# Fused channel attention and FFN on one core: the read-back of lines of maxima and the additions behind W_in loads are put a period later

## The chip, the cores and the metric

One core of a Trainium2 chip. The metric is device time in microseconds (us) of one execution; three runs of the kernel before have a median of 2120.12 us. Lower is better.

## What is computed

q, k and v have the shape (4, 6080, 256); W_in is 256 x 2048, W_out 2048 x 256, both stored as float64, and the outputs are compared in float32. The reference, cut:

```python
qn = q / (norm(q, axis=1) + 1e-6); kn = k / (norm(k, axis=1) + 1e-6)
s = kn.transpose(0, 2, 1) @ qn / tau          # (4, 256, 256)
a = softmax(s, axis=-1)
x = (v @ a).reshape(24320, 256)               # tokens
h = x @ w_in
return maximum(0.01 * h, h) @ w_out
```

The kernel doesn't form x: for each batch b it multiplies the small matrix a into W_in (`w_pair`), and then sends v through that product, the leaky step and W_out.

## The kernel before

**Tiles and periods.** The tokens of a batch are cut into six tiles (`NT`) of twice 512 or twice 496 tokens, 24 tiles in all. For each tile i, the main loop at the end of the kernel runs over eight pairs p of blocks of the 2048 hidden columns. One pass of its body is a period; the number of the period, i * 8 + p, stands in `now[0]`. In each period TensorE makes the products of one pair (`block_product` into the banks `ps_x`, `ps_y`, `ps_z`; a Strassen-Winograd scheme of seven block products, each split in three passes of high and low parts), and in between, in pieces by `out(5)`, `out(5)`, `out(8)` and the remaining six, the 24 products with W_out of the period before (`ffn_out`, bank `ps_o`). ScalarE copies sums out of the banks (`taken`, L827), makes the leaky step and the high halves (`leaky`, L809 and L812); VectorE adds into `h` (`add`, L821) and makes the low halves (L814). At the end of a tile four results `o_sb` are copied (L864) and stored to `out_dram` on SyncE (L874).

**The order of the work.** `in_order` pins the order of TensorE, ScalarE and VectorE to that in which the Python code calls the operations. Side work goes through queues: `at(w, fn)` has a function called at the start of period w; `put(queue, length, fn, then)` appends an operation to an engine's list `todo`; `slot(queue, room)` lets waiting operations into a gap of the period, first in first out, as far as their lengths fit the room. `put_steps` chains operations: each is put when the one before it has been issued; an entry "call" only calls a function. An entry for "act_next" reaches ScalarE's list at the start of the next period. DMAs on SyncE are not pinned: the framework's scheduler orders that queue when the program is compiled, and SyncE then works through it in this order, waiting in front of each DMA for what it needs.

**Lines of maxima (`Scale`).** From period 40 on, the operands are float16, scaled by a power of two. For this the greatest magnitude is needed: `see` gives it per partition (L141), and `gather` (L146 to L149) reduces it to a column of 128 values, writes the column to a line in DRAM and reads the line back, broadcast to all partitions, into a buffer `all`. `find` (L154 on) makes the scales of it. There are twenty such lines: one of `wo_scale` (found in period 24), one of `w_scale` (gathered at the end of the second `sums_work`, found in period 33) and eighteen of `v_scale` (`v_scale_work`: for tile i + 1 gathered in the second period of tile i and found at the start of its fourth).

**Sums of W_in blocks (`sums_work`).** In period 9 for q = 0 and in period 17 for q = 1, four blocks of W_in are loaded from DRAM (`win_in`, L962), added and subtracted on VectorE (`whole` L974, `minus` L981), their maxima taken (`seen`), split in high and low (`halves`: L986 on ScalarE, L990 on VectorE) and stored to `win_sums` (L991); later periods use them in `w_pair`. A first pair of blocks is loaded when `sums_work` is called, which puts the steps in the same breath; a second pair by `more`, behind the low half of block 0.

**Shared buffers.** `win` tiles, the chunks `qk_raw` of queries and keys, and the converted weights share a ring of four buffers with the tag "raw" (`RBUFS`). In periods 8 to 27 the chunks of batch 1 pass through it, to be squared on ScalarE (L217) and added up on VectorE (L220). `h`, `o_sb`, `all`, `sq` and others share twelve buffers with the tag "temp" (`TEMPS`); a buffer of `o_sb` comes free when its store has landed.

Of the kernel before, what the change touches and what calls it, by code (L numbers as in the profile page):

```python
# [36 lines left out]
def channel_attention_ffn(  # L37
# [29 lines left out]
    if N % TILE:  # L67
        rest = N % TILE // 2 + (widths.pop() if widths else 0)
# [18 lines left out]
    def temp(dtype=F32, name="temp"):  # L87
        return work.tile([P, TW], dtype, name=name, tag="temp", bufs=TEMPS)
# [32 lines left out]
    def f32(ap):  # L121
        return ap if ap.dtype == F16 else ap.bitcast(F32)
# [5 lines left out]
    class Scale:  # L128
# [16 lines left out]
        def gather(self):  # L145
            last = nc.vector.tensor_reduce(out=self.top, in_=self.most, axis=AX.X, op=ALU.max)  # L146
            nc.sync.dma_start(out=self.line, in_=self.top)
            self.all = temp(name="all")[:, 0:P]
            nc.sync.dma_start(out=self.all, in_=self.line.rearrange("p o -> (p o)").partition_broadcast(P))  # L149
            return last  # L150

        def find(self):
            e = self.e.bitcast(I32)
# [16 lines left out]
    class Scores:  # L170
# [10 lines left out]
        def begin(self, acc, *s):  # L181
            self.acc, self.s = acc, s
# [333 lines left out]
    def flat(w):  # L516
        return f32(w.rearrange("p x f -> p (x f)"))
# [40 lines left out]
    def w_tmp(name):  # L558
        return work.tile([P, TW], F32, name=name, tag="w_tmp", bufs=8)
# [7 lines left out]
    now, w_done, w_stores = [0], {}, []  # L567
# [315 lines left out]
    def at(w, fn, *args):  # L883
        steps.setdefault(w, []).append((fn, args))
# [10 lines left out]
    def put(queue, length, fn, then=(), first=False, ready=lambda: True):  # L895


        def run():
            ins = fn()
            for entry in then:  # L900
                if entry[0] == "call":
                    entry[1](*entry[2:])
                else:
                    put(*entry)
            return ins

        run.ready = ready
        (todo[queue].appendleft if first else todo[queue].append)((length, run))
# [51 lines left out]
    def win_in(src):  # L960
        r = win_tile(False)
        nc.sync.dma_start(out=flat(r), in_=src)  # L962
        return r

    def sums_work(q):

        blocks = {(h, x): win_in(win_dram[2 * q + x][h]) for h, x in ((0, 1), (0, 0))}
        t = {}

        def whole(name, h, x):  # L970
            def fn():
                r = blocks[h, x]
                t[name] = w_tmp("win_s")
                return nc.vector.tensor_tensor(out=t[name], in0=f32(r[:, 0, :]), in1=f32(r[:, 1, :]), op=ALU.add)  # L974
            return ("dve", 0.7, fn)

        def seen(h, x):
            return ("dve", 0.7, lambda: w_scale.see(f32(blocks[h, x][:, 0, :])))

        def minus(out, x, y):  # L980
            return ("dve", 0.7, lambda: nc.vector.tensor_tensor(out=t[out], in0=t[x], in1=t[y], op=ALU.subtract))  # L981

        def halves(name, x):
            def high():
                t[name, 0] = work.tile([P, 2, TW], F32R, name="win_t", tag="qk_split", bufs=3)
                return nc.scalar.copy(out=t[name, 0][:, 0, :], in_=t[name])  # L986

            def low():
                r = t[name, 0]
                ins = nc.vector.tensor_tensor(out=r[:, 1, :], in0=t[name], in1=f32(r[:, 0, :]), op=ALU.subtract)  # L990
                nc.sync.dma_start(out=win_sums[q][x], in_=flat(r))  # L991
                return ins
            return [("act_next", 0.65, high), ("dve", 0.7, low)]

        def more():
            for h, x in ((1, 1), (1, 0)):
                blocks[h, x] = win_in(win_dram[2 * q + x][h])

        put_steps([
            whole("a", 0, 1), seen(0, 1), whole("b", 0, 0), seen(0, 0), minus("b", "a", "b"), *halves("b", 0),  # L1000
            ("call", more),
            whole("c", 1, 1), seen(1, 1), minus("a", "c", "a"), *halves("a", 2), minus("c", "c", "b"),
            *halves("c", 1), whole("d", 1, 0), seen(1, 0), minus("d", "d", "c"), *halves("d", 3),
            *([("dve", 0.2, w_scale.gather)] if q else []),
        ], False, False)

    A_S1, A_S2, A_S3, A_S4, A_11, A_12, A_22 = range(7)

# [87 lines left out]
    def put_steps(steps, first, on=True):  # L1096

        def entry(n):
            then = [entry(n + 1)] if n + 1 < len(steps) else ()
            if steps[n][0] == "call":  # L1100
                return ("call", lambda: (steps[n][1](*steps[n][2:]), *(put(*x) for x in then)))
            return (*steps[n], then, first or n > 0 and on)

        put(*entry(0))
# [70 lines left out]
    for pair in range(NWC // 2):  # L1175
        at(9 + 8 * pair, sums_work, pair)
# [196 lines left out]
    last = None  # L1373
    for i in range(NTILES):
        for p in range(NPAIR):
# [14 lines left out]
            if last is not None:  # L1390
                leaky(i, p - 1, "C12", last, last)
                last = None
# [41 lines left out]
            else:  # L1434
                last = h12
# [33 lines left out]
```

## Time and profile before

| | us |
|---|---|
| median of 3 runs | 2120.12 |
| the runs, from to | 2119.97 to 2120.28 |
| the profiled execution, device time | 2117.38 |
| its span, first to last instruction | 2115.6 |
| TensorE busy | 2093.8 |
| VectorE busy | 1594.4 |
| ScalarE busy | 1473.1 |

The times of all rows below are from the one profiled execution and count from the start of its span. PE is TensorE, DVE VectorE, ACT ScalarE, SPq the DMA queue of SyncE. A line of the timeline gives the start, the duration, the engine, the line of the code, the operation and its tiles, and in brackets how long the engine was idle before it and for whom it waited. A wait is given to the releaser that came last.

### The profile page before, as it was taken

The numbers are of one execution on the slowest core, as the hardware profiler recorded it, in microseconds if no ns is written. First come the engines' busy times: TensorE is split into PE (matmuls) and PEld (weight loads), VectorE is DVE, ScalarE is ACT, GpSimd is POOL, SyncE is SP. The second block draws the span as 40 slices with busy tenths as digits, with TensorE's granted clock in tenths as the row PEclk, the third lists the DMA queues.
The fourth block names the chain that finished last, engine by engine and source line by source line (L and its number), as shares of the span: only waits on it lengthen the run. The fifth ranks groups of instructions, "written<-read, shape, count | busy, mean of one in ns | idle before, by whom it ended". The sixth has DMA issues, their size and how long they took to land.

```text
span 2115.6 us, 27081 instructions
## 1 busy us (share of the span) xinstructions
PE 2093.8 (99%) x9656; PEld 1214.5 (57%) x9656; DVE 1594.4 (75%) x2905; ACT 1473.1 (70%) x2571; POOL 3.3 (0%) x11
## 2 busy tenths in 40 slices
PE   9999999999999999999999999999999999999999
PEld 8887877788875555544444545554444444444444
DVE  7988887777788777877878877777788766666654
ACT  6576777666667777766667777776666666666666
POOL 0000000000000000000000000000000000000000
PEclk9999999999999999999999999999999999999999
DMA  9946665444643333322534333232343222222220
GB/s 363 395 169 204 205 232 191 165 149 160 219 143 104 116 114 105 102 102 86 174 112 135 114 105 115 95 111 73 125 150 99 82 77 80 65 84 72 65 72 29
DMA packets 120167, 283.46 MB, mean 134 GB/s; under 512 B 15072, under 2 KB 40160, under 8 KB 120032
## 3 DMA queue, kind: packets, MB, share of 16 engines
q1 hardware_dynamic: 119664, 281.41, 39.2%
q8 instruction: 76, 1.25, 0.3%
q14 instruction: 59, 0.48, 0.1%
q10 hardware_dynamic: 368, 0.32, 0.1%
HBM read 227.93 MB, written 53.75 MB: 133 GB/s over the span
## 4 chain that ended last, share of the span: by engine, by line
PE 86%; DVE 7%; ACT 5%; DMA 1%; issue 1%; ACTq 0%
PE ps_o L847 40%; PE ps_x L798 21%; PE ps_z L798 15%; PE ps_s L250 4%; DVE h L821 2%; PE ps_o L250 2%; ACT h L809 2%; ACT g_split L812 2%; DVE g_split L814 2%; PE ps_y L250 2%; PE ps_s L1030 1%; ACT h L827 1%; DVE v_split L754 1%; DMA win<-win_dram 0%; DMA out_dram<-o_sb 0%
## 5 line engine op out<-in xcount | busy, mean ns | idle before, releaser
L847 PE MATMUL ps_o<-g_split,w_out_split 128*128 128x512 f16 (+3 forms) x4608 | 1124.7, 380 | 0.0
L814 DVE TENSOR_TENSOR g_split<-h,g_split 128x512 f16<-128x512 f32 (+3 forms) x768 | 524.9, 684 | 285.4 <-ACT g_split L812 270.6
L798 PE MATMUL ps_x<-v_split,w_split 128*128 128x512 f16 (+3 forms) x2304 | 628.0, 381 | 7.2 <-ACT h L827 6.8
L809 ACT ACTIVATE h<-h 128x512 f32<-128x512 f32 (+1 forms) x576 | 360.9, 627 | 326.6 <-DVE h L821 326.4
L847 PEld LDWEIGHTS <-w_out_split 128*128 128x128 f16 x3456 | 337.9, 98 | 400.2
L821 DVE TENSOR_TENSOR h<-ps_z,h 128x512 f32<-128x512 f32 (+1 forms) x568 | 386.6, 681 | 191.4 <-ACT h L827 185.7
L827 ACT COPY h<-ps_x 128x512 f32<-128x512 f32 (+1 forms) x576 | 333.2, 579 | 230.7 <-PE ps_x L798 221.9
L798 PEld LDWEIGHTS <-w_split 128*128 128x128 f16 x3024 | 288.4, 98 | 356.5 <-issue 37.1
L812 ACT CAST g_split<-h 128x512 f16<-128x512 f32 (+3 forms) x768 | 471.9, 615 | 23.6
L798 PE MATMUL ps_z<-v_split,w_split 128*128 128x512 f16 (+3 forms) x1680 | 456.3, 380 | 8.2 <-DVE h L821 6.6
L847 PEld LDWEIGHTS ps_o<-g_split,w_out_split 128*128 128x128 f32 x1152 | 217.2, 189 | 44.2
L798 PEld LDWEIGHTS ps_x<-v_split,w_split 128*128 128x128 f32 x576 | 107.9, 189 | 29.7 <-ACT h L827 7.4
L809 ACT ACTIVATE h<-ps_x 128x512 f32<-128x512 f32 (+1 forms) x192 | 112.8, 587 | 7.0 <-PE ps_x L798 6.6
L220 DVE TENSOR_TENSOR sq_acc<-sq_acc,sq 128x512 f32<-128x512 f32 x141 | 96.5, 684 | 0.4
L798 PEld LDWEIGHTS ps_z<-v_split,w_split 128*128 128x128 f32 x408 | 76.1, 189 | 24.2 <-DVE h L821 9.5
L217 ACT ACTIVATE sq<-qk_raw 128x512 f32<-128x512 f32 x141 | 87.2, 630 | 0.0
L754 DVE SCALAR_TENSOR_TENSOR v_split<-v_raw,v_scale,v_split 128x512 f16<-128x512 f32 (+1 forms) x107 | 79.8, 746 | 3.8
L250 PE MATMUL ps_s<-qk_split 128*128 128x512 f32 x192 | 73.2, 391 | 0.0
L229 DVE TENSOR_TENSOR qk_split<-qk_raw,qk_split 128x512 fp32r<-128x512 f32 x96 | 65.6, 684 | 0.0
L250 PE MATMUL ps_y<-qk_split 128*128 128x512 f32 x192 | 60.4, 337 | 0.0
L225 ACT CAST qk_split<-qk_raw 128x512 fp32r<-128x512 f32 x96 | 59.0, 615 | 0.0
L752 DVE TENSOR_SCALAR v_split<-v_raw,v_scale 128x512 f16<-128x512 f32 (+1 forms) x107 | 51.0, 477 | 0.0
(165 smaller groups left out, 1024.7 us busy)
## 6 DMA issues: line engine op xcount, KB each, us to landing
w_split<-w_dram SPq DMA_DIRECT2D x144, 448.0 KB, 3.9
w_split<-w_dram SPq DMA_DIRECT2D x40, 896.0 KB, 4.7
qk_raw<-in_q_dram SPq DMA_DIRECT2D x115, 256.0 KB, 4.8
qk_raw<-in_k_dram SPq DMA_DIRECT2D x115, 256.0 KB, 5.4
v_raw<-in_vT_dram SPq DMA_DIRECT2D x32, 512.0 KB, 4.8
out_dram<-o_sb SPq DMA_DIRECT2D x64, 256.0 KB, 4.4
win<-win_dram SPq DMA_DIRECT2D x26, 512.0 KB, 3.6
win<-win_sums SPq DMA_DIRECT2D x24, 512.0 KB, 3.3
```

What stands on the lines that cost most here:

```text
L217: return nc.scalar.activation(out=out, in_=self.chunk(j), func=AF.Square)
L220: return nc.vector.tensor_tensor(out=self.acc[0], in0=self.acc[0], in1=sq, op=ALU.add)
L229: return nc.vector.tensor_tensor(out=sp[:, :, 1, :], in0=self.chunk(j), in1=f32(sp[:, :, 0, :]), op=ALU.subtract)
L250: mm = nc.tensor.matmul(out=out, lhsT=lhsT, rhs=rhs, start=start, stop=stop, skip_group_check=True)
L754: return nc.vector.scalar_tensor_tensor(out=sp[:, 1, 0:w], in0=src, scalar=up, in1=sp[:, 0, 0:w], op0=ALU.mult, op1=ALU.subtract)
L798: mm = nc.tensor.matmul(out=ps[:, 0:n], lhsT=w[:, x, a, :], rhs=sp[:, y, 0:n], start=first and k == 0, stop=k == 2, skip_group_check=True,)
L809: nc.scalar.activation(out=out[:, 0:n], in_=h[:, 0:n], func=AF.Prelu, alpha=0.01, scale=G_SCALE if i >= T16 else 1.0)
L812: issued["act"] = nc.scalar.copy(out=sp[:, 0, 0:n], in_=out[:, 0:n])
L814: issued["dve"] = nc.vector.tensor_tensor(out=sp[:, 1, 0:n], in0=out[:, 0:n], in1=f32(sp[:, 0, 0:n]), op=ALU.subtract)
L821: issued["dve"] = nc.vector.tensor_tensor(out=h[:, 0:n], in0=ps[:, 0:n], in1=h[:, 0:n], op=ALU.add)
L827: issued["act"] = nc.scalar.copy(out=h[:, 0:n], in_=ps[:, 0:n])
L847: issued["pe"] = nc.tensor.matmul(out=o_ps[i][j][h][:, 0:n], lhsT=wo_lhsT(i, x, f, h), rhs=sp[:, y, 0:n], start=p == 0 and early and k == ...
```

## The change

Two edits. In `Scale`, the read-back of a line leaves `gather` and becomes a function `read` of its own, which is called at the start of the period after the one in which `gather` was issued. In `sums_work`, the loads of the first pair stay where they are, but the steps on it are put at the start of the next period (`begin`); the loads of the second pair (`more`) are called right behind the second `seen`, and the steps on that pair (`rest`) are put at the start of the period after the one in which the low half of block 0 was issued. The steps themselves and their order are the same.

```diff
@@ -145,9 +145,12 @@
         def gather(self):
             last = nc.vector.tensor_reduce(out=self.top, in_=self.most, axis=AX.X, op=ALU.max)
             nc.sync.dma_start(out=self.line, in_=self.top)
+            at(now[0] + 1, self.read)
+            return last
+
+        def read(self):
             self.all = temp(name="all")[:, 0:P]
             nc.sync.dma_start(out=self.all, in_=self.line.rearrange("p o -> (p o)").partition_broadcast(P))
-            return last
@@ -996,13 +999,18 @@
-        put_steps([
-            whole("a", 0, 1), seen(0, 1), whole("b", 0, 0), seen(0, 0), minus("b", "a", "b"), *halves("b", 0),
-            ("call", more),
+        def begin():
+            put_steps([
+                whole("a", 0, 1), seen(0, 1), whole("b", 0, 0), seen(0, 0), ("call", more),
+                minus("b", "a", "b"), *halves("b", 0), ("call", lambda: at(now[0] + 1, put_steps, rest, False, False)),
+            ], False, False)
+
+        rest = [
             whole("c", 1, 1), seen(1, 1), minus("a", "c", "a"), *halves("a", 2), minus("c", "c", "b"),
             *halves("c", 1), whole("d", 1, 0), seen(1, 0), minus("d", "d", "c"), *halves("d", 3),
             *([("dve", 0.2, w_scale.gather)] if q else []),
-        ], False, False)
+        ]
+        at(now[0] + 1, begin)
```

## Rows read from the trace of the kernel before

**Rows 1.** Page, part 1: TensorE's busy us (share of the span), instructions.

```profile
PE 2093.8 (99%) x9656; PEld 1214.5 (57%) x9656; DVE 1594.4 (75%) x2905; ACT 1473.1 (70%) x2571; POOL 3.3 (0%) x11
```

**Rows 2.** Waits of TensorE, whole span: us in total, times, longest us.

```profile
PE ps_x L798 <- ACT h L827: 6.8, 3, 6.0
PE ps_z L798 <- DVE h L821: 6.6, 7, 2.6
```

**Rows 3.** Timeline of TensorE: the eight `ps_o` products, once in each period.

```profile
194.56 1.98 PE L847 MATMUL ps_o<-g_split,w_out_split 128*128 128x512 f32 x8
207.72 2.00 PE L847 MATMUL ps_o<-g_split,w_out_split 128*128 128x512 f32 x8
217.94 1.98 PE L847 MATMUL ps_o<-g_split,w_out_split 128*128 128x512 f32 x8
...
279.29 1.98 PE L847 MATMUL ps_o<-g_split,w_out_split 128*128 128x512 f32 x8
292.23 2.00 PE L847 MATMUL ps_o<-g_split,w_out_split 128*128 128x512 f32 x8
...
365.19 1.98 PE L847 MATMUL ps_o<-g_split,w_out_split 128*128 128x512 f32 x8
384.31 1.98 PE L847 MATMUL ps_o<-g_split,w_out_split 128*128 128x512 f32 x8
```

**Rows 4.** Windows: stretch, us, each engine's busy us, granted clock, DMA share, GB/s.

```profile
372.50:379.00 6.50, 5.86 (x14) 4.59 (x15) 4.66 (x7) 4.20 (x7) 0.00 (x0) 0.51 0.72 262
```

**Rows 5.** Chain that ended last, in three stretches: start us, us, what.

```profile
191.39 6.41 DMA win<-win_dram
...
278.96 3.94 DMA win<-win_dram
...
362.97 9.46 DMA out_dram<-o_sb
```

**Rows 6.** Timeline of VectorE: steps of `sums_work`, and `gather` of `w_scale`.

```profile
191.59 0.68 DVE L974 TENSOR_TENSOR win_s<-win 128x512 f32<-128x512 f32 x1
197.82 0.69 DVE L974 TENSOR_TENSOR win_s<-win 128x512 f32<-128x512 f32 x1 [3.51 <-DMA win<-win_dram]
208.03 0.68 DVE L990 TENSOR_TENSOR win_t<-win_s,win_t 128x512 fp32r<-128x512 f32 x1
...
352.67 0.15 DVE L146 TENSOR_REDUCE w_scale<-w_scale 128x1 f32<-128x8 f32 x1
```

**Rows 7.** Timeline of ScalarE, 352 to 382 us: the first `o_sb`, the late `h`.

```profile
357.91 0.58 ACT L864 COPY o_sb<-ps_o 128x512 f32<-128x512 f32 x1
...
372.51 0.59 ACT L827 COPY h<-ps_x 128x512 f32<-128x512 f32 x1 [7.15 <-DMA out_dram<-o_sb]
```

**Rows 8.** Timeline of SyncE's DMA queue: a second-pair load; the line of `w_scale`.

```profile
199.14 0.33 SPq L962 DMA_DIRECT2D win<-win_dram  x1
...
352.85 0.33 SPq L147 DMA_DIRECT2D w_scale_line<-w_scale  x1
362.08 0.33 SPq L149 DMA_DIRECT2D all<-w_scale_line  x1
...
362.97 3.15 SPq L874 DMA_DIRECT2D out_dram<-o_sb  x3
```

**Rows 9.** Timeline of SyncE's DMA queue: a chunk's load, a `v_scale` read-back.

```profile
216.10 0.33 SPq L198 DMA_DIRECT2D qk_raw<-in_q_dram  x1
...
985.31 0.33 SPq L149 DMA_DIRECT2D all<-v_scale_line  x1
```

**Rows 10.** Timeline of ScalarE: squares of chunks of batch 1.

```profile
226.48 1.15 ACT L217 ACTIVATE sq<-qk_raw 128x512 f32<-128x512 f32 x2
```

**Rows 11.** Page, part 6: issues, KB each, median us from issue to landing.

```profile
all<-v_scale_line SPq DMA_DIRECT2D x18, 64.0 KB, 5.4
```

**Rows 12.** Tile `out_dram`, 185 to 195 us: the landing of four stores.

```profile
DMA to landing us min/median/max: 6.3/6.5/6.7
```

**Rows 13.** Timeline of VectorE: the `find` that reads the line of 985.31.

```profile
992.34 0.28 DVE L154 TENSOR_REDUCE v_scale<-all 128x1 f32<-128x128 f32 x1
```

## The prediction

> **What bounds the kernel now.** I read the page's busy times first. TensorE is busy for 2093.8 us, 99% of the span [rows 1]; no edit here takes an instruction from it, so only its idle time and its slow stretches can be won: some 22 us at most. Next, its waits [rows 2]: 6.8 us in 3 waits on ScalarE's copies of `ps_x`, 6.0 of it in one, and 6.6 us in 7 waits on VectorE's additions to `h`, 2.6 the longest. To see where these lie and what they cost in all, I took the TensorE timeline and one mark in each period: the start of the eight `ps_o` products, which every period has once. An ordinary period is 217.94 - 207.72 = 10.22 us. Three are longer [rows 3]: 13.16 (194.56 to 207.72), 12.94 (279.29 to 292.23) and 19.12 us (365.19 to 384.31). Over the ordinary period that is 2.94, 2.72 and 8.90, together 14.56 us. I price by marks and not by the waits, because the third wait of 6.0 us costs 2.9 more than itself: right behind it the granted clock is 0.51, the lower level, for 6.5 us [rows 4]; the first two waits have no such tail. The periods are numbered as in `now[0]`: tile 1 begins with period 8, and the three are 9, 17 and 25.
>
> Then each of the three followed back, with the chain of waits [rows 5] and the timelines of the engines.
>
> Periods 9 and 17: in both, the chain goes through the landing of the second `win` load of `sums_work`. It is issued at 191.39 and lands at 197.80; in period 17, at 278.96 and 282.90 [rows 5]. VectorE runs its queue in a fixed order. It has the first addition `win_s` done at 191.59, comes to the second and stands 3.51 us for the load [rows 6]; behind it stand the additions to `h`, for which `ps_z` and so TensorE wait. The pair of loads is called in the very period of the additions.
>
> Period 25: ScalarE stands 7.15 us before a copy to `h`, for a `temp` buffer whose store of `o_sb` hasn't landed [rows 7]. That store was issued at 362.97 [rows 8] and landed at 372.43 [rows 5], though its first `o_sb` was copied by 357.91 + 0.58 = 358.49 [rows 7]. Between, the DMA queue of SyncE was parked: the line of `w_scale` was written at 352.85, its read-back waited behind it until 362.08 for that write to land, and the stores stood behind the read-back [rows 8]. So one line in twenty costs time, because it falls on a tile's end.
>
> **The loads a period ahead.** The first pair keeps its place in the text, period 9 (17); the additions are put into VectorE's queue one period later. Nothing is computed more or less: 0 us of work. In the period after, the first addition comes at about 191.59 + 10.22 = 201.8, and the load is in at 197.80: 4 us to spare. In period 17, the mark of 18 without the stall is 279.29 + 10.22 = 289.5, the addition 3 us before it (as 191.59 is before 194.56), so 286.5 against 282.90: 3.6 us to spare. Both waits go: -2.94 and -2.72. The second pair is called after the second `seen`, and its users follow one period after `low` of block 0, so it's ahead too; it makes no wait now.
>
> What the move costs is in the ring of four `raw` buffers, which `win` shares with the query and key chunks of batch 1. Two `win` tiles now keep their buffers a period longer, and the second two between one and two. No row prices that. From below it is nothing: the loads go into buffers that squares free. From above: the load at 216.10 [rows 9] goes out as the second pair's first buffer comes free; it lands some 3.9 us later by the nearest row [rows 5], and the next pair of squares starts at 226.48 [rows 10], so there are 6.4 us of slack. Moved by 10.22, the load is 3.8 us late if those squares are its own. TensorE sees 1.2 less than ScalarE (7.15 against 6.0 [rows 2, 7]): 2.6 us, twice (two sums), 5.2. I take a quarter, 1.3, since buffers freed by squares should serve most of these loads. Less than nothing is out: no load comes earlier by it. The chain of sums ends with `w_scale.gather`, now one or two periods later; its reader, `w_scale.find`, is held back to period 33, eight periods on, so nothing waits there.
>
> **The lines a period later.** `read` is called at the start of the next period: one DMA each, twenty in all, none added. SyncE should be free between write and read-back. For eighteen of them (the `v_scale` lines, [rows 11]) I take 0: their parking stands in front of loads that are called three periods ahead, and TensorE has no wait that goes back to it. For `w_scale` two things help: `gather`, at 352.67 now [rows 6], falls a period later, behind the stores of period 25, and its `read` is a period after that. The stores go out from 358.49 on. At a tile's end with nothing parked they land in 6.5 us [rows 12], at 365.0; ScalarE wanted the buffer at 372.51 - 7.15 = 365.36 [rows 7]. So the wait goes; -8.90, with the clock's tail. If it wants the buffer of the last store, copied some 2.5 us later, it stands about 2.4 us, TensorE 1.3 at most: I add half, 0.65. Who is next in line? Ordinary periods, in which TensorE doesn't wait.
>
> The Trainium skill ("DMA: Bandwidth & Descriptors", "Anatomy of one DMA") puts a DMA's fixed cost at about 2.0 us and the rest at its bytes. By that the line of 0.5 KB would be back in 2 us, the queue free long before the stores were ready, and only the 5.66 us of the loads could be won; the row, 9.23 us from write to read-back, contradicts it, and the measurement decides.
>
> **The sum**: -2.94 - 2.72 - 8.90 + 1.3 + 0.65 = -12.6 us. The profiled execution took 2117.4 us (span 2115.6), 2.7 below the median of 2120.12; from it the sum gives 2104.8, and from the median 2107.5, which I forecast.
>
> **Rivals.**
> (a) The lines don't move. SyncE's queue order in the trace isn't the text's: the second pair's first load is issued at 199.14 [rows 8], though the text calls it behind a `low` that runs at 208.03 [rows 6]. A `read` called later may be compiled into the same place, parked again, and the stall of some tile's stores stays, in period 25 or as much elsewhere. Then the loads alone count: 2120.1 - 5.7 + 1.3 = 2115.7. Against it: `gather` itself moves, and any one period has a tile's end only one time in eight.
> The same skill page ("Two DMAs through the same engine are not ordered") asks that the second of such a pair wait for the first's completion, so wherever `read` is placed, its wait goes along.
> (b) No change: the waits on the loads come back as waits of the same length on late chunks (2120).
> (c) Slower, by the `raw` ring. If the second pair is held two periods longer, not one, and the load at 216.10 goes into its buffer for the squares at 226.48, it lands at 216.10 + 20.4 + 3.9 = 240.4, and ScalarE, whose order is fixed, stands 14.0 us. TensorE stands 12.8, plus the clock's tail of 2.9 as in period 25: 15.7, twice. -14.6 + 31.4 gives 2120.1 + 16.8 = 2137. It decides from some 7.3 us a sum on, or about a period and a half. For it: the call of `rest` at a period's start can add most of a period to the one of `begin`. Against it: 6.4 us of slack, and squares free a buffer in every period.
> (d) The read-back is late for its `find`. At a narrow tile the read goes out at 985.31 [rows 9], `find` starts at 992.34 [rows 13], and a landing takes 5.4 us [rows 11]: 1.6 us to spare. If it were 3 us later at all eighteen, `find` would stand 1.4 us; of 3.51 us of waiting on VectorE 2.94 became period, so 0.8 us each, 14 in all: 2107.5 + 14 = 2122, no change. For it: `read` comes behind the next period's loads. Against it: those are ready only at a period's end, and most tiles should have more room.
>
> **How the numbers follow.** Forecast 0.60 (2105 to 2112); (a) 0.16; (b) 0.05; (c) 0.11; (d) 0.08, of which a half is slight and still faster. About 0.2%, 4.2 us, is what a measurement of this kernel can tell from no change: faster is under 2115.9. (a) lies on that line; I count 0.10 of its 0.16 as faster. Faster 0.60 + 0.10 + 0.04 = 0.74; same 0.06 + 0.05 + 0.03 = 0.14; slower 0.12. The range: below, all three stalls with no new cost, 2105.6, and a little of the other idle time, 2103; above, it has to reach through (a) and (b), 2121, which leaves (c) and a part of (d) out.
>
> **What would show it.** Right: marks of periods 9, 17 and 25 10.2 to 11 us apart; no wait of VectorE on `win_dram` and none of ScalarE on `out_dram` above 1 us; no stretch at the lower clock near 370 us. In SyncE's queue other DMAs stand between a line's write and its read-back. Wrong: a wait of ScalarE on `qk_raw` in periods 10 to 14 or 18 to 24 (the ring), of VectorE's `find` on `all`, or stores parked again behind a line. The forecast falls if one of these is over 8 us in all.

## The result and the profile after

The changed kernel takes 2102.23 us (2101.90 to 2102.85, 4 runs) against 2120.05 us (2118.45 to 2120.28) for the one before: a ratio of 0.9918, 95% interval 0.9906 to 0.9931. It is 17.8 us faster. The profiled executions are 2117.38 before and 2102.85 after, 14.5 us apart.

The waits of TensorE after, on `ps_x` and `ps_z` (engine, line, waited for: us in total, times, longest), stand against [rows 2]:

```profile
PE ps_z L801 <- DVE h L824: 1.4, 4, 0.5
PE ps_x L801 <- ACT h L830: 0.9, 2, 0.4
```

13.4 us have become 2.3, with none above 0.5. The marks of the periods after, on the timeline of TensorE, stand against [rows 3]:

```profile
195.79 1.98 PE L850 MATMUL ps_o<-g_split,w_out_split 128*128 128x512 f32 x8
205.99 1.98 PE L850 MATMUL ps_o<-g_split,w_out_split 128*128 128x512 f32 x8
...
277.73 2.00 PE L850 MATMUL ps_o<-g_split,w_out_split 128*128 128x512 f32 x8
287.95 1.98 PE L850 MATMUL ps_o<-g_split,w_out_split 128*128 128x512 f32 x8
...
349.15 1.98 PE L850 MATMUL ps_o<-g_split,w_out_split 128*128 128x512 f32 x8
359.69 2.00 PE L850 MATMUL ps_o<-g_split,w_out_split 128*128 128x512 f32 x8
369.91 1.98 PE L850 MATMUL ps_o<-g_split,w_out_split 128*128 128x512 f32 x8
```

Periods 9, 17 and 25 are 10.20, 10.22 and 10.22 us: all three stalls are gone whole. Period 24 is 10.54 us; before, it ran from the mark below to the one at 365.19 of [rows 3], 11.74 us, which the prediction passed over.

```profile
353.45 1.98 PE L847 MATMUL ps_o<-g_split,w_out_split 128*128 128x512 f32 x8
```

VectorE after, against [rows 6]: the two first additions of `sums_work`, and `gather` of `w_scale`.

```profile
205.67 0.69 DVE L977 TENSOR_TENSOR win_s<-win 128x512 f32<-128x512 f32 x1
...
213.34 0.69 DVE L977 TENSOR_TENSOR win_s<-win 128x512 f32<-128x512 f32 x1
...
402.54 0.15 DVE L146 TENSOR_REDUCE w_scale<-w_scale 128x1 f32<-128x8 f32 x1
```

SyncE's queue after, against [rows 8]: the second load of the first pair, the four stores at the end of tile 2, the line of `w_scale`, and the first line of `v_scale`.

```profile
192.62 0.33 SPq L965 DMA_DIRECT2D win<-win_dram  x1
...
352.94 2.60 SPq L877 DMA_DIRECT2D out_dram<-o_sb  x4
...
402.72 0.32 SPq L147 DMA_DIRECT2D w_scale_line<-w_scale  x1
409.72 0.32 SPq L153 DMA_DIRECT2D all<-w_scale_line  x1
...
531.87 0.32 SPq L147 DMA_DIRECT2D v_scale_line<-v_scale  x1
539.01 0.32 SPq L153 DMA_DIRECT2D all<-v_scale_line  x1
```

Three things are to be seen. The load of 192.62 is used at 213.34, 20.7 us later, and no wait stands before either addition. The stores go out at once, with no line in front of them. And the lines are parked as before: 7.0 us for `w_scale`, 7.1 for the first `v_scale`, with nothing in between. What has moved is the gather itself, from 352.67 to 402.54, five periods.

### The profile page after: what moved, and what is told of

Same layout as the page of the kernel before. It is cut to its first block, busy times and chain, and to the rows that moved or that the text cites. A ratio compares the mean times of both kernels' runs of the same rounds, so it can differ in the third digit from the quotient of the medians.

```text
span 2101.1 us, 27083 instructions
## 1 busy us (share of the span) xinstructions
PE 2089.8 (99%) x9656; PEld 1213.3 (58%) x9656; DVE 1593.8 (76%) x2905; ACT 1472.5 (70%) x2571; POOL 3.3 (0%) x11
## 4 chain that ended last, share of the span: by engine, by line
PE 87%; DVE 6%; ACT 4%; DMA 2%; issue 1%; SPq 0%; ACTq 0%; DVEq 0%
PE ps_o L850 42%; PE ps_x L801 22%; PE ps_z L801 16%; PE ps_s L253 3%; DVE h L824 2%; ACT h L812 2%; ACT g_split L815 2%; PE ps_y L253 2%; DVE g_split L817 1%; PE ps_s L1038 1%; DMA qk_raw<-in_k_dram 1%; DMA qk_raw<-in_q_dram 1%; DVE v_split L757 1%; PE ps_y L556 0%; ACT h L830 0%
```

## The experiments

**Each edit alone.** `e1_sums_only` is the changed kernel with the read-back put back:

```diff
         def gather(self):
             ...
             nc.sync.dma_start(out=self.line, in_=self.top)
-            at(now[0] + 1, self.read)
-            return last
-
-        def read(self):
             self.all = temp(name="all")[:, 0:P]
             nc.sync.dma_start(out=self.all, in_=self.line...partition_broadcast(P))
+            return last
```

> The edit of the sums alone; each line is read back right behind its write, as before. Theory A (place): the third stall went because the chain of sums ends later, so that the line of w_scale no longer falls on a tile's end; the edit of the lines does nothing. Then this gives all of the change, 2102 us (2101 to 2104). Rival B (read-back): the third stall went because the read-back was taken from behind the write; then periods 9 and 17 are ordinary here, but a stall of stores stays somewhere, 2102 + 9 = 2111 us.

Measured: 2102.16 us (2101.79 to 2102.38), ratio 0.9913 (0.9896 to 0.9929). The edit of the sums alone gives the whole change. Its `gather` of `w_scale` writes its line at 402.13 us.

`e2_lines_only` is the reverse: the kernel before, with `read` called a period after `gather`.

> The edit of the lines alone; the sums as before, gather of w_scale still in period 24 beside the tile's end. Theory A: the compiled queue holds the read-back behind its write as before, all three stalls stay, 2120 us. Rival B: the third stall goes with its 8.9 us and perhaps the 1.2 us of period 24, 2110 us; periods 9 and 17 stay at 13 us.

Measured: 2114.32 us (2112.17 to 2118.32), ratio 0.9973 (0.9962 to 0.9984), between the two expectations. Its SyncE queue at the end of tile 2:

```profile
354.07 0.33 SPq L147 DMA_DIRECT2D w_scale_line<-w_scale  x1
358.47 0.33 SPq L653 DMA_DIRECT2D w_split<-w_dram  x1
359.37 0.81 SPq L877 DMA_DIRECT2D out_dram<-o_sb  x2
364.56 0.33 SPq L153 DMA_DIRECT2D all<-w_scale_line  x1
364.98 0.69 SPq L877 DMA_DIRECT2D out_dram<-o_sb  x1
```

and its ScalarE:

```profile
369.97 0.59 ACT L830 COPY h<-ps_x 128x512 f32<-128x512 f32 x1 [3.51 <-DMA out_dram<-o_sb]
```

Here the later call does something: one load of weights and two of four stores pass ahead of the read-back, which still parks the queue until 364.56. ScalarE's wait for a store is 3.51 us and not the 7.15 of [rows 7]. By the marks of this profile period 25 is 12.96 us, 2.7 over an ordinary one in place of 8.9. So the edit of the lines takes most of the third stall where `gather` stays at the tile's end; in the changed kernel it doesn't stay there.

**How much a stall differs from one execution to the next.** `e3_before_again` is the kernel before, unchanged.

> The kernel before, unchanged, profiled once more. The profiled execution of before took 2117.4 us, 2.7 under its median, that of after 0.6 over its median. If the third stall differs from execution to execution (its length, or how long the clock stays at the lower level), this profile shows period 25 at another length than 19.1 us and the execution near 2120 us. If profiled executions of this kernel are always shorter, it shows 2117 us and 19.1 us again.

Measured: 2120.21 us (2117.64 to 2122.20, 10 runs), ratio 1.0001 (0.9992 to 1.0010). The profiled execution took 2121.23 us, 3.9 more than the one of the prediction. Its marks:

```profile
195.54 1.98 PE L847 MATMUL ps_o<-g_split,w_out_split 128*128 128x512 f32 x8
210.15 1.98 PE L847 MATMUL ps_o<-g_split,w_out_split 128*128 128x512 f32 x8
...
281.71 1.98 PE L847 MATMUL ps_o<-g_split,w_out_split 128*128 128x512 f32 x8
296.59 1.98 PE L847 MATMUL ps_o<-g_split,w_out_split 128*128 128x512 f32 x8
...
369.52 2.01 PE L847 MATMUL ps_o<-g_split,w_out_split 128*128 128x512 f32 x8
388.10 1.98 PE L847 MATMUL ps_o<-g_split,w_out_split 128*128 128x512 f32 x8
```

Periods 9, 17 and 25 are 14.61, 14.88 and 18.58 us, where [rows 3] have 13.16, 12.94 and 19.12. Over an ordinary period of 10.22 that is 17.4 and not 14.56. Two windows behind the first two waits show why (stretch, us, busy us of PE, PEld, DVE, ACT, POOL, granted clock, DMA share, GB/s):

```profile
201.80:205.00 3.20, 3.20 (x9) 2.55 (x8) 2.30 (x5) 2.52 (x5) 0.00 (x0) 0.50 0.86 289
...
287.20:290.30 3.10, 2.94 (x7) 2.37 (x8) 2.94 (x6) 2.69 (x5) 0.00 (x0) 0.50 0.44 120
```

and the same stretches behind the waits in the first execution of before:

```profile
200.90:204.10 3.20, 3.20 (x16) 2.62 (x15) 2.29 (x5) 2.93 (x7) 0.00 (x0) 1.00 0.83 281
...
284.50:287.60 3.10, 3.10 (x14) 2.51 (x14) 2.94 (x6) 2.79 (x6) 0.00 (x0) 1.00 0.51 173
```

In 3.2 us at the lower level TensorE makes 9 products, at the upper 16. The first wait is as long in both, 2.50 us here:

```profile
200.69 0.96 PE L798 MATMUL ps_z<-v_split,w_split 128*128 128x512 f32 x3 [2.50 <-DVE h L821]
```

and 2.55 us in the first execution of before:

```profile
199.77 0.96 PE L798 MATMUL ps_z<-v_split,w_split 128*128 128x512 f32 x3 [2.55 <-DVE h L821]
```

The second wait is itself longer here, 3.00 us against 2.33.

So the same first wait costs 2.94 us in one execution and 4.39 in another, as the clock falls behind it or not. The Trainium skill ("TensorE: Matmul & The Clock Gate", "Terms") puts the price of such a stretch at its length times the share of the clock's pulses that are held back. By that the 3.2 us shown cost 1.6 us, an estimate; the two executions are 1.45 us apart in this period, which agrees.

**The place of the line.** `e4_gather_later` is the kernel before, with the one line of `w_scale` gathered two periods later:

```diff
-            *([("dve", 0.2, w_scale.gather)] if q else []),
+            *([("call", lambda: at(now[0] + 2, put, "dve", 0.2, w_scale.gather))] if q else []),
```

> Before with one change: the gather of w_scale is put two periods later than the last step of the sums; loads, additions and read-back as before. Theory A: the parked read-back no longer stands in front of the stores of period 25: that period is ordinary, and 8.9 us and up to 1.2 us of period 24 go: 2110 us, with periods 9 and 17 still at 13 us. If the stores are late for another reason (the 12 buffers, the traffic of period 24), 2120 us.

Measured: 2109.86 us (2109.42 to 2111.23), ratio 0.9951 (0.9936 to 0.9966). The marks from period 24 on:

```profile
354.31 1.98 PE L847 MATMUL ps_o<-g_split,w_out_split 128*128 128x512 f32 x8
365.99 1.98 PE L847 MATMUL ps_o<-g_split,w_out_split 128*128 128x512 f32 x8
376.19 1.98 PE L847 MATMUL ps_o<-g_split,w_out_split 128*128 128x512 f32 x8
```

Period 25 is ordinary; 24 is as long as before, 11.68 us. So the third stall is the line in front of the stores, and it is worth about 10 us on the median; the excess of period 24 is something else. (The line is parked here too, for 8.8 us from 363.99 on, behind the stores, and costs nothing.)

**What made period 24 long.** Of before, one more line of ScalarE's waits: its fixed order has `wo`, the first step on ScalarE that scales W_out, in front of a copy to `h`, and `wo` stands 1.8 us for VectorE.

```profile
ACT wo L680 <- DVE wo_whole L679: 2.1, 2, 1.8
```

`e10_weights_later` is `e4_gather_later` with these steps a period later (`at(25 + n, ...)` in place of `at(24 + n, ...)` for `wo_half`).

> As e4_gather_later (109.9 us over 2000), and the steps that scale W_out (wo_half) are begun in period 25 in place of 24. Theory: the 1.2 to 1.5 us that period 24 took over an ordinary one came from ScalarE's fixed order, in which the first wo stood 1.8 us for wo_whole ahead of a copy to h; a period later it falls between others and period 24 is 10.4 us: 2108.5 us. Rival (the work of a tile's end and the find of wo_scale make period 24 long): it stays at 11.7 us, 2110 us.

Measured: 2110.74 us (2109.25 to 2111.89), ratio 0.9954 (0.9939 to 0.9969): no gain in the median. Its wait on `wo_whole` and the marks of period 24 are:

```profile
ACT wo L680 <- DVE wo_whole L679: 0.3, 1, 0.3
```

```profile
356.00 1.98 PE L847 MATMUL ps_o<-g_split,w_out_split 128*128 128x512 f32 x8
366.36 1.99 PE L847 MATMUL ps_o<-g_split,w_out_split 128*128 128x512 f32 x8
```

Period 24 is 10.36 us: the marks show that these steps made it long. That it was their wait on `wo_whole`, and not the rest of their work, is the reading that fits: in the changed kernel they begin in period 24 as before, but `wo` stands for nothing there (its one such wait, 0.9 us, comes at 399 us), and the period is 10.54 us. The time doesn't show the 1.3 us. In the two profiled executions period 9 takes them back: it is 14.43 us here (the granted clock is 0.62 over 201.0 to 204.3 us) and 13.14 in that of `e4_gather_later`. The runs here spread over 2.6 us.

**One line of the sums' edit.** `e5_first_pair` is the kernel before, with the steps put a period later and nothing else:

```diff
-        put_steps([
+        at(now[0] + 1, put_steps, [
             whole("a", 0, 1), seen(0, 1), whole("b", 0, 0), seen(0, 0), ...
```

> Before with the steps of sums_work put one period after the call, all else as before: the second pair is loaded and used right behind low of block 0, lines read back in gather. Theory: the waits of periods 9 and 17 are the second load's landing and nothing else, so both periods become 10.2 us, -6 to -9 us by the two profiled executions of before; the gather moves by a period or more, and if it leaves the tile's end, period 25 is ordinary too: 2102 us; if it stays in front of the stores, 2111 us. Rival: the second part of the edit (the second pair and the steps behind it) is needed against waits on the second pair; then VectorE waits for win_dram in period 11 or 19, 2105 us or more.

Measured: 2101.96 us (2101.78 to 2103.50), ratio 0.9919 (0.9902 to 0.9935). `win_dram` isn't among VectorE's waits; the `w_scale` line is written at 402.41 us. This one line gives the whole gain, since it also moves `gather` off the tile's end: the second pair and `rest`, and the edit of the lines, add nothing that can be measured.

**The line put back.** `e6_line_at_end` is `e1_sums_only` with a line more, of ones, that no result uses:

```diff
+    idle_scale = Scale("idle_scale", 8)
+    def idle_gather():
+        nc.vector.memset(idle_scale.most, 1.0)
+        return idle_scale.gather()
+    def idle_used():
+        return nc.vector.tensor_reduce(out=idle_scale.e, in_=idle_scale.all, axis=AX.X, op=ALU.max)
+    at(24, put, "dve", 0.2, idle_gather)
+    at(28, put, "dve", 0.3, idle_used)
```

> The edit of the sums alone (2102 us) and, on top, one more line of 128 ones, gathered in period 24 just before the find of wo_scale, read back right behind its write, used in period 28. Theory (a line parked at a tile's end holds the stores up): ScalarE waits for out_dram in period 25, the period is 5 to 9 us longer, 2107 to 2112 us. Rival (the line matters only together with the rest of period 24 of before): 2102 to 2103 us.

Measured: 2107.62 us (2107.30 to 2108.57), 5.5 us over `e1_sums_only`; by the marks period 25 is 15.50 us. The queue and ScalarE:

```profile
348.31 0.33 SPq L147 DMA_DIRECT2D idle_scale_line<-idle_scale  x1
356.68 0.33 SPq L149 DMA_DIRECT2D all<-idle_scale_line  x1
357.10 0.38 SPq L650 DMA_DIRECT2D w_split<-w_dram  x1
357.58 4.14 SPq L874 DMA_DIRECT2D out_dram<-o_sb  x4
```

```profile
367.13 0.63 ACT L217 ACTIVATE sq<-qk_raw 128x512 f32<-128x512 f32 x1 [4.48 <-DMA out_dram<-o_sb]
```

`e13_line_at_end_split` has the edit of the lines on top of that (`read` as in the changed kernel).

> As e6_line_at_end (2107.6 us), with the edit of the lines as well. Theory: as in e2_lines_only, some of the stores of the tile's end pass ahead of the read-back and the stall in period 25 shrinks to 3 us or less: 2102 to 2105 us. Rival: no change, 2107 to 2108 us.

Measured: 2103.55 us (2103.29 to 2104.41). Of the 5.5 us, 4.1 go: the weights' load and one store pass ahead of the read-back, and ScalarE's wait for a store is 1.3 us. So the edit of the lines does what it is for where a line falls on a tile's end.

**Is it only the tile's end?** `e7_line_in_middle` is `e6_line_at_end` with `at(20, ...)` and `at(24, ...)`.

> The same line of ones in period 20, the middle of a tile, where no store is due. Both theories of the place: SyncE is parked some 7 us and nothing waits for it, 2102 to 2103 us. If parking costs time wherever it is (late chunks, late weights), 2105 us or more.

Measured: 2106.33 us (2104.28 to 2107.24), 4.2 over `e1_sums_only`: not what I held. VectorE's list let it through only at 309.99, right before the line of `wo_scale`; with both parked one after the other, until 329.57, ScalarE stood 3.85 us for a chunk of batch 1. I took it to be the pair, and put one line alone elsewhere: `e11_single_line_mid`, with `at(18, ...)` and `at(22, ...)`.

> As e7_line_in_middle, but the line of ones is gathered some two periods earlier, so that it isn't followed at once by the line of wo_scale. Theory: one parking of 7 to 9 us away from a tile's end is covered, 2102 us within 1; it was two in a row that made a chunk late. Rival: any extra parking in the periods of the squares costs, 2104 us or more.

Measured: 2108.73 us (2106.55 to 2109.39), 6.6 over `e1_sums_only`. That fell too. The queue and ScalarE:

```profile
287.53 0.32 SPq L147 DMA_DIRECT2D idle_scale_line<-idle_scale  x1
294.58 0.32 SPq L149 DMA_DIRECT2D all<-idle_scale_line  x1
295.00 0.38 SPq L198 DMA_DIRECT2D qk_raw<-in_q_dram  x1
295.43 0.42 SPq L198 DMA_DIRECT2D qk_raw<-in_k_dram  x1
```

```profile
301.82 0.63 ACT L217 ACTIVATE sq<-qk_raw 128x512 f32<-128x512 f32 x1 [5.82 <-DMA qk_raw<-in_k_dram]
```

The chunk's load, which in the changed kernel goes out at 287.6 us, is held until 295.00, and its square comes 5.8 us late. So a single parking can cost as much in the middle of a tile, while chunks pass through the `raw` ring. In this profiled execution, the fastest of its four, period 19 is 14.10 us, 3.9 over an ordinary one, with the clock at its upper level behind the wait. It depends on what is due: the line of `wo_scale` in the kernel before (7.4 us from 322.98 on) and that of `w_scale` in `e4_gather_later` were parked among the chunks too, and neither shows in the marks.

`e12_two_lines_split` is `e7_line_in_middle` with the edit of the lines.

> As e7_line_in_middle (2106.3 us), with the edit of the lines as well: each read-back is called at the start of the next period. Theory: the call lets other DMAs that are due pass ahead of the read-back, so the chunk is in time and most of the 4 us go: 2102 to 2104 us. Rival: the queue is compiled in the same order and parked as long: 2106 us.

Measured: 2104.80 us (2103.69 to 2108.52), against 2104.28 to 2107.24 without the edit. The ranges overlap: not told apart by the time. The profiles show that the stall is still there: ScalarE's wait on the chunk is 3.5 us, 3.85 without the edit, and period 23 is 14.36 us, 14.61 without it.

**The eighteen lines.** `e9_lines_on_pool` is the changed kernel with `nc.gpsimd.dma_start` for both DMAs of `Scale`.

> The changed kernel with write and read-back of all twenty lines issued by GpSimd's queue in place of SyncE's; SyncE is never parked for a line. Theory (the eighteen v_scale lines cost nothing): 127 us of waits leave SyncE's queue and the time stays, 2102 us within 1. If their parking holds weights or chunks up, faster by 2 us or more; if the landing by the other queue is slower than the 1.5 periods to find, VectorE waits and it is slower by 0.8 us for each us of wait and line.

Measured: 2102.05 us (2101.88 to 2102.36). SyncE is never parked for a line, and the time is the same. The parking of the `v_scale` lines is free.

## Why the prediction was right and wrong

The time, 2102.23, lies 0.8 us under the range and 5.3 under the forecast. Point by point:

- **The three places and their mechanisms: right.** Periods 9 and 17 were the landing of the second load (`e5_first_pair`), 25 the line in front of the stores (`e4_gather_later`, and `e6_line_at_end` as the reverse). All are ordinary after.
- **The size of the stalls: the step that failed.** The sum put the three stalls at 14.56 us, read from one execution, and subtracted that from the median of others, though the prediction said that this execution lay 2.7 us under the median. Its "the first two waits have no such tail" was true of this execution and taken for the kernel: in `e3_before_again` the clock falls behind both, and the same three periods hold 17.4 us of stall. Of the 3.85 us between the two executions 2.85 lie in these periods, the other 1.0 ahead of the mark of period 1 (102.32 against 101.33). Taken from its own execution each sum comes out, with the 1.2 us of period 24 (below): 2117.38 - 14.56 - 1.2 = 2101.6 and 2121.23 - 17.4 - 1.2 = 2102.6, on both sides of the measured 2102.23. How much stall the runs without a profile had isn't shown. The runs of the changed kernel lie within 1.0 us, the ten of `e3_before_again` were spread over 4.6: with the stalls most of the spread has gone.
- **The two added costs: nothing.** The `raw` ring, put at 1.3 us, and the stores, put at 0.65, cost nothing: ScalarE waits neither for a `qk_raw` chunk of batch 1 nor for `out_dram` in the profile after. These are 1.95 of the 5.3 us by which the forecast was too high; the rest is the stalls and period 24.
- **Period 24: left out.** It was 1.5 us too long and became 10.54; 1.2 us came from there. In the profiled execution after, it is made up for at the start, where the first mark, that of period 1, comes 1.2 us later than before (102.56 against 101.33), after waits of 0.3 us for a chunk's load and 0.6 for the sums of squares. That mark moves between executions of one kernel too, as said above. So that 2117.38 - 14.56 = 2102.8 falls on the 2102.85 of the profiled execution after is luck: two differences of 1.2 us cancel.
- **What the edit of the lines does: wrong for this kernel.** I gave it half of the third stall's end. The sums' edit alone moves `gather` out of the way (`e1_sums_only`). Rival (a) holds as far as the queue goes: in the changed kernel nothing passes between write and read-back of `w_scale`, as shown above, nor at sixteen of the eighteen lines of `v_scale` (one load at each of the other two, three DMAs at the line of `wo_scale`), so the sign that the prediction named is all but missing. But a gather at a tile's end is helped (`e2_lines_only`, `e13_line_at_end_split`).
- **The chain of sums: one or two periods later was said, five it is.** It did no harm, since `find` is in period 33, where `gather` now comes in 29. `e5_first_pair`, without `rest`, ends at the same place, so it isn't `rest`. The timeline of VectorE shows how the lag grew in the second sum: 23.8 us at the low half of block 0 (317.84 against 294.01 before) and 52.5 at that of block 3 (400.39 against 347.93). In between, from 350.58 on, the steps that scale W_out run on the same two engines; before, the first of them came at 353.56, behind `gather`. Two periods were enough (`e4_gather_later`); that it became five, behind the squares and short of the next tile's end, was luck.
- **Eighteen lines free: right** (`e9_lines_on_pool`). **That a line costs only at a tile's end: wrong** (`e11_single_line_mid`). Rival (a) leaned on that with "one time in eight"; in the periods of the squares, of four cases in which a line was parked in front of chunks, two cost nothing (`wo_scale` before, `w_scale` in `e4_gather_later`) and two (`e7_line_in_middle`, `e11_single_line_mid`) 4 to 7 us.
- **Rivals (c) and (d): not seen.** Nothing waited for the moved loads or for chunks behind them, though `e11_single_line_mid` shows how little it takes: a load 7.4 us late there costs 3.9 us in the profiled execution and 6.6 in the median. No `find` waited for `all`.

## What to carry to other kernels

Subtract what you read in one execution from that execution's time; if it lies below the median, ask whether the difference is more of the same stall. Where an engine with a fixed order waits for a load, put its use a whole period behind the issue before anything else: here one such line was the change, and the Trainium skill's rule ("DMA: Bandwidth & Descriptors", "Rules for kernel authors"), to issue early and wait late, is borne out by the load of 192.62 that is used at 213.34. A DMA that waits for another's landing holds up all that is queued behind it, so look at what is due in those 7 us, stores and loads of chunks alike.

## What the runs showed of the hardware

The granted clock fell to the lower level (0.50) behind waits of TensorE of 2.43, 2.50 and 3.0 us, and stayed at the upper one (1.00) behind others of 2.33 to 3.1: of the ten waits of periods 9 and 17 in five profiled executions (before, `e2`, `e3`, `e4`, `e10`) three were followed by a slow stretch, and the length of the wait didn't decide. In the other profiles it fell behind a wait of 2.23 us (`e12`) and stayed at the upper level behind one of 3.46 (`e11`). The read-back of a line of 0.5 KB could go out only 6.1 to 12.7 us after its write on SyncE's queue. On GpSimd's the write landed in 7.9 us in the median of the eighteen, on SyncE's in 7.4 before and 7.8 after: the other queue made it no sooner.
